# Three maxima products of a cycle in one phase, in the lead of a fused attention and gMLP block

## The chip, the cores and the metric

The kernel runs on one core of a Trainium2 chip. The metric is the time of one execution on the device, in microseconds (us), as the median of several runs. Engines are named as in the profile: PE (matrix products; PEld is its weight loads), DVE (vector), ACT (scalar and activation), POOL (general vector), SP (here only an issuer of DMAs). Each engine works off its own instructions in order; a DMA queue belongs to the engine that issues it.

## What is computed

`x` has 2048 rows of 512. After a layer norm, two branches are computed from it and added to `x`: attention with 32 heads of 16 columns, and a gMLP.

```python
xn = layernorm(x)
qkv = (xn @ wqkv).reshape(B, S, 3, 32, 16)            # q, k, v
p = softmax(einsum("bhqd,bhkd->bhqk", q, k) * 16**-0.5)
A = einsum("bhqk,bhkd->bhqd", p, v).reshape(B, S, 512) @ wo
z = gelu(xn @ w_in); z1, z2 = z[..., :896], layernorm(z[..., 896:])
B_ = (z1 * (einsum("ts,bsf->btf", w_sp, z2) + b_sp)) @ w_out
return x + A + B_
```

## The kernel before

**Numbers in two parts.** Most float32 products are taken as three matmuls of a high and a low part (`mm3`, lines 170 to 172). A high part is a rounding copy on ACT, a low part a subtraction on DVE or POOL; the pair lies in one tile.

**Attention, two heads at a time.** There are 16 head pairs p. Stacks `qst` and `kst` hold the 48 rows of both heads in two halves of the partitions (two heads' matmuls go side by side). For each pair, the softmax needs the row maximum of the scores. So each score is computed twice: once in a *maxima product* (`max_mm`, tile `mx`, L650) with queries on the partitions, which DVE reduces (`max_red`, L658, tile `mm`), and once as a *score tile* (`scores`, tile `st`, L955) with keys on the partitions, in which two more rows of the stacks subtract the maximum; ACT takes the exponential from it (`exp`, tile `pf`), and `pv` multiplies by v (L929). After 16 maxima products `max_fin` (lines 660 to 684) combines their maxima in five small DVE operations into `ms`; `ms` is written to DRAM (`mscr`) by a DMA, and four DMAs load it from there into the rows of `qst`. `mx` and `st` tiles share three accumulator tags, `s0` to `s2`, in turn (`spsum`).

**Phases.** After a prologue (norms, v, the projections of the first four head pairs) the main loop runs over *phases*, the variable `half` in the code. Two phases make a cycle of three score tiles and three maxima products; the maxima run ahead of the scores by LEAD = 27 products. Hence a *lead*: phases -18 to -1, in which there are maxima products only. The first score tile comes in phase 0. In each phase the loop does, in this order:

- `flush()`: DMAs that were put off with `later(k, ...)`, k phases ago, are issued, in the order in which they were put off. They go to SP's queue.
- the score tiles and maxima products of the phase on PE; the exponentials and part of `pv`
- DMAs in `behind` (the writes of `ms`), on ACT's queue
- `max_red` of the phase's products; in even phases `max_fin` of those three products which the counter has reached
- if a group of projection products has ended in the last phase (`drain`): one step of its generator, which copies the accumulator (`qr`, on ACT)
- one step of each generator in `bg`, and of each in `side`, but of `side` only while `load["D"]`, the planner's account of DVE's work, is not above `limit`
- units of the background queue (`qk_rest`, `z2_all`, `z1_all`, ...), four in a phase of the lead (`credit = 2600`, a unit costs 650); later only in odd phases, with a credit that spreads the rest evenly up to score tile 931.

The limit and the account, at the place where the maxima are reduced; `dve(1024)` adds 0.065 + 1024/960 to `load["D"]`:

```python
limit = load["D"] + (2.5 if half % 2 == 0 else 3.0)
for m in ms:
    max_red(m)
...
side[:] = [g for g in side if load["D"] > limit or next(g, 0) is None]
```

**The background of the lead.** `qk_rest` projects q and k for the later head pairs: for each of four row groups g and three column blocks m, a *group* of 12 matmuls for q (a = 0) and one for k (a = 1), four units each. In the lead, groups use two accumulator banks in turn, tags `d` and `o`; from phase -2 on a new (m, g) uses `d` alone. ACT copies a finished group to `qr` (one of four tiles). Then `qk_split` (lines 319 to 330) goes on as a generator in `side`. Its steps: 1. the high part, ACT, into a new tile `hilo` (profile: `qkhl`), of which there are three; 2. the low part, POOL (L325); 3. once the planner's clock for POOL says that this is done, the store to `qscr` or `kscr` is put off by one phase, to SP's queue. A tile is free for its next use when its store has landed. When m = 3 begins, the four xnT pieces of the next row group are fetched by SP (`fetch_xnT`, 512 KB each). The weights of m = 2 and 3 are loaded and split on POOL by the generator `prepare` in `bg`, which hands a weight over when the planner's clock (2.7 per phase) has reached the planner's account of POOL; until then a phase has no group.

Order on every engine is the order in which the code is traced (a schedule by hand); waits are put in for data and for free tiles.

Of the kernel before, what the change touches and what calls it, by code (L numbers as in the profile page):

```python
# [33 lines left out]
LEAD = 27  # L34
# [6 lines left out]
def fused_block(ctx, tc, x, wqkv, wo, w_in, w_spT, b_sp, w_out, out):  # L41
# [48 lines left out]
    mscr = [dr.tile([4, 32, 32], F32, name=f"mscr{i}") for i in range(4)]  # L90
# [16 lines left out]
    now = [-2 * LEAD // 3 - 1]  # L107
# [18 lines left out]
    def later(k, fn, *args):  # L126
        late.append((now[0] + k, fn, args))
# [4 lines left out]
    def flush():  # L132
        due = [l for l in late if l[0] <= now[0]]
        late[:] = [l for l in late if l[0] > now[0]]
        for _, fn, args in due:
            fn(*args)
# [478 lines left out]
    def load_stacks(p, cols=slice(0, S)):  # L615
        m, r = p // 4, (p % 4) * 2
        q, k = qst[p % 2], kst[p % 2]
        sl = [slice((r + j) * DH, (r + j + 1) * DH) for j in range(2)]
        for j in range(2):
            for i, (t, scr) in enumerate(((q, qscr), (k, kscr))):  # L620
                two = t[64 * j:64 * j + 2 * DH, cols], scr[m][sl[j], :, cols]
                one = t[64 * j + 2 * DH:64 * j + KS, cols], scr[m][sl[j], i, cols]
                for args in (two, one):
                    if p and 2 * j + i:
                        later(2 * j + i, move, *args)
                    else:
                        move(*args)
# [4 lines left out]
    behind = []  # L632
# [19 lines left out]
    def max_red(i):  # L652
        if i >= NSTEP:
            return
        p, c, t, kc = step_of(i)
        if i % 16 == 0:
            mmax[i // 16] = at.tile([P, 2, 4, 4], F32, tag="mm", name=f"mm{i // 16}", bufs=2)
        dve(1024).tensor_reduce(mmax[i // 16][:, :, t, kc], mstep.pop(i), AX.X, ALU.max)  # L658

    def max_fin(i):  # L660

        if i < 0 or i >= NSTEP or i % 16 != 15:
            return
        g = i // 16
        p, c = divmod(g, 4)


        mm = mmax.pop(g)
        mn = at.tile([P, 2, 4, 2], F32, tag="mn", name=f"mn{g}", bufs=1)
        mr = mrow[:, 0:16].rearrange("p (j a t) -> p j a t", j=2, a=2)  # L670
        nc.vector.tensor_reduce(mr[:, :, 0, :], mm, AX.X, ALU.max, negate=True)
        nc.vector.tensor_reduce(mn[:, :, :, 0], mm, AX.X, ALU.max, negate=True)
        nc.vector.tensor_reduce(mn.bitcast(F32R)[:, :, :, 1], mm, AX.X, ALU.max)
        with nc.allow_low_precision(reason="the second of two parts, of which the first is exact"):
            nc.vector.tensor_reduce(mr[:, :, 1, :], mn, AX.X, ALU.add)
        ms = at.tile([P, 32], F32, tag="ms", name=f"ms{g}", bufs=2)
        nc.vector.transpose(ms, mrow.bitcast(F32))
        load["D"] += 0.6
        behind.append((now[0] + 1, mscr[g % 4].rearrange("b k x -> (b k) x"), ms))
        for j in range(2):  # L680
            for a in range(2):
                row = 64 * j + KS + a
                k = 4 * (2 * j + a)
                later(2, move, qst[p % 2][row:row + 1, c * 512:(c + 1) * 512], mscr[g % 4][:, k:k + 4, :].rearrange("b t x -> t b x"))
# [121 lines left out]
    def last_mm(t, on):  # L806

        acc = spsum(f"al{t}")
        for a in range(2):
            u = slice(32 * (t % 4 + a), 32 * (t % 4 + a) + 32)  # L810
            nc.tensor.matmul(acc[:, a, :], on[u, :], sel["ones"][u, 1, :], start=True, stop=True)
        return t, acc

    def last_add(t, acc):
        f = fin[t // 2]
        dve(1024).tensor_add(f, acc, f)
        move(out[t * P:(t + 2) * P, :].rearrange("(a p) d -> p a d", p=P), f)
# [9 lines left out]
    def init_rows(a):  # L827

        for j in range(2):
            row = 64 * j + KS  # L830
            for r in range(2):
                nc.gpsimd.dma_start(raw(kst[a])[row + r:row + r + 1, :], cscr[0:1, :])

    engines = {mybir.EngineType.PE, mybir.EngineType.Activation, mybir.EngineType.DVE, mybir.EngineType.Pool, mybir.EngineType.SP}
    with tc.manual_schedule(engines=engines):
# [136 lines left out]
        def exp(n):  # L972
            pf = at.tile([P, 1024], F32, tag="pf", name=f"pf{n}", bufs=PF)
            act(pf, sts.pop(n).rearrange("p j q -> p (j q)"), AF.Exp, 1024, scale=0.25)
            full[n] = pf

        def chunk_out(p, c):
            e = t512(f"e{p}_{c}")
            acc = accs.pop((p, c))
            if (p, c) == order[-1][:2]:  # L980
                act(e[:, 0:256], acc[:, 0:256], AF.Copy, 256)
                dve(256).tensor_copy(e[:, 256:], acc[:, 256:])
            else:
                act(e, acc, AF.Copy, 512)
            if p == NP - 1:
                later(2, lambda: urgent.append(last_pair(c, e)))
                return
            i = (p % 4) * 2
            later(1, move, escr[p // 4][c][i:i + 2].rearrange("j r w d q -> (j r w d) q"), e)
            if p % 4 == 3 or p == NP - 2:  # L990
                later(2, lambda: bg.append(norm_out(p // 4, c)))
# [3 lines left out]
        for half in range(-2 * LEAD // 3, 2 * (N // 3 + 4)):  # L995
            b = 3 * (half // 2)
            ms = [b + LEAD] if half % 2 == 0 else [b + LEAD + 1, b + LEAD + 2]
            ns = [n for n in ([b, b + 1] if half % 2 == 0 else [b + 2]) if 0 <= n < N]
            now[0] = half
            flush()  # L1000
            for n in ns:
                if n == 16:
                    init_rows(1)
                if n % 64 == 14 and n // 64 + 1 < NP:
                    load_stacks(n // 64 + 1)
            pause = max(0, pause - 1.5)
            final = []
            if b + LEAD >= NSTEP and half % 2 and turn and turn[0][0] + 1 in added:
                final.append(last_mm(*turn.pop(0)))
            tiles = [(scores, n) for n in ns]  # L1010
            for i, m in enumerate(ms):
                tiles.insert(1 if half % 2 == 0 else 2 * i, (max_mm, m))
            for make, n in tiles:
                make(n)
            while ended:
                chunk_out(*ended.pop(0))
            for n in ns[:1]:
                exp(n)
            if half % 2 == 0:
                pv_some(b - 1, ready // 2 * 2)  # L1020
            for n in ns[1:]:
                exp(n)
            while behind and behind[0][0] <= half:
                nc.scalar.dma_start(*behind.pop(0)[1:])
            for f in final:
                last_add(*f)
            low = min(load.values())
            for e in load:
                load[e] = min(load[e] - low, 2.0)
# [4 lines that stand above are left out]
            if half % 2 == 0:  # L1034
                for m in range(ms[0] - 2, ms[0] + 1):
                    max_fin(m)
            if drain:
                drain = False
                cost = next(queue[0], None)
                if cost is None:  # L1040
                    queue.pop(0)
                else:
                    pause = -cost
            bg[:] = [g for g in bg if next(g, 0) is None]
            side[:] = [g for g in side if load["D"] > limit or next(g, 0) is None]
            ready += len(ns)
            if b < 0:
                credit = 2600
            elif half % 2:
                credit = min(credit + 3 * (max(todo / max(DENSE - b, 10), 600 if b > DENSE - 15 else 0) if todo > 0 else max((todo + 64 * 650) / max(N - 6 - b, 8), 450)), 3250)  # L1050
            else:
                continue
            if urgent and between and not drain and "ones" in sel:
                queue.insert(0, urgent.pop(0))
                pause = 0
            took = 0
            while queue and not pause and not drain and go():
                cost = next(queue[0], None)
                if cost is None:
                    queue.pop(0)  # L1060
                elif cost <= 0:
                    pause = -cost
                else:
                    drain = between = cost % 1 > 0
                    credit -= cost
                    todo -= cost
                    left[0] -= 1
                    took += 1
# [38 lines left out]
```

## Time and profile before

| | |
|---|---|
| median of 3 runs | 1958.39 us (1957.21 to 1958.47) |
| profiled execution: its own time | 1960.21 us |
| profiled execution: span, first to last instruction | 1958.4 us |
| PE busy | 1938.7 us, 99% of the span |
| DVE, ACT, POOL busy | 1373.7, 1232.5, 725.5 us |
| first maxima product, first score tile | 85.91, 140.44 us |

The page gives for each engine its busy time and share of the span, and the chain of waits: what ended last, followed back. A row of a timeline has the start, the duration (us), the engine (SPq and ACTq are DMA issues), the line, the operation with its output and inputs, how many were merged into the row, and in brackets the idle time of the engine before it and what ended this. A row of the windows view has the length of the stretch, the busy time and count of each engine, the granted clock of PE (1.00 is full), the share of the DMA engines' time, and GB/s. Matmuls overlap, so the difference of two starts says more than one's duration.

### The profile page before, as it was taken

Reading aid. Unit: us, or ns where it says so; the run is one execution under the profiler, and the core shown is the slowest. Engines: PE = TensorE matmul, PEld = TensorE weight load, DVE = VectorE, ACT = ScalarE, POOL = GpSimd, SP = SyncE. Lnnn points to the kernel's source line nnn. Section 1 sums busy time; section 2 is a strip of 40 time slices with the busy share of each in tenths; the row PEclk is TensorE's granted clock in tenths of the full one; section 3 lists DMA queues with packets and bytes.
Section 4 is the critical chain, followed back from the end, with each engine's and each line's share of the span. In section 5 each row is a group of like instructions: output and inputs, shape, how many; then the busy total and the mean of one; then the engine's idle time right before and its main releaser. Section 6 shows DMA issues by size and latency. Waiting matters only on the chain.

```text
span 1958.4 us, 32641 instructions
## 1 busy us (share of the span) xinstructions
PE 1938.7 (99%) x12559; PEld 1049.7 (54%) x12559; DVE 1373.7 (70%) x1565; ACT 1232.5 (63%) x1407; POOL 725.5 (37%) x790
## 2 busy tenths in 40 slices
PE   8999999999999999999999999999999999999998
PEld 7765555555555555555555555555555555555543
DVE  5356777777767677777777767777777777777872
ACT  4347778888677666656566656665666655556664
POOL 3334278889776931026122531017112400002100
PEclk9999999999999999999999999999999999999999
DMA  7566344363535535365545745346454645355323
GB/s 260 201 219 183 104 120 117 111 179 107 144 132 153 183 117 141 101 166 156 142 137 162 202 131 134 104 120 205 110 158 144 180 140 137 106 147 160 105 73 113
DMA packets 229202, 284.23 MB, mean 145 GB/s; under 512 B 35176, under 2 KB 134136, under 8 KB 226168
## 3 DMA queue, kind: packets, MB, share of 16 engines
q1 hardware_dynamic: 217240, 272.64, 47.9%
q0 software_dynamic: 2592, 8.46, 1.1%
q10 hardware_dynamic: 9216, 1.05, 0.4%
q8 instruction: 99, 1.62, 0.3%
q14 instruction: 55, 0.45, 0.1%
HBM read 188.51 MB, written 93.58 MB: 144 GB/s over the span
## 4 chain that ended last, share of the span: by engine, by line
PE 95%; DVE 2%; ACT 1%; issue 1%; DMA 0%; POOL 0%; SPq 0%; DVEq 0%; ACTq 0%
PE o L929 23%; PE mx L650 16%; PE st L955 15%; PE sp L170 7%; PE sp L172 5%; PE sp L171 5%; PE mo L170 2%; PE qk L170 2%; PE z1p L170 2%; PE z2p L170 2%; PE qk L171 1%; PE qk L172 1%; PE mo L171 1%; PE mo L172 1%; PE z1p L172 1%; PE z1p L171 1%
## 5 line engine op out<-in xcount | busy, mean ns | idle before, releaser
L658 DVE TENSOR_REDUCE mm<-mx 128x2 f32<-128x1024 f32 x1024 | 1221.9, 1222 | 498.2 <-PE mx L650 493.9
L58 ACT ACTIVATE pf<-st 128x1024 f32<-128x1024 f32 x1024 | 1028.8, 1025 | 620.0 <-PE st L955 591.6
L929 PE MATMUL o<-pf,vall 128*32 128x512 f32 (+1 forms) x5120 | 511.0, 513 | 0.0
L650 PE MATMUL mx<-kst,qst 48*128 48x512 f32 x2048 | 446.7, 434 | 2.7 <-ACT pf L58 1.8
L955 PE MATMUL st<-qst,kst 50*128 50x512 f32 x2048 | 445.2, 431 | 1.3 <-DVE mm L658 1.1
L650 PEld LDWEIGHTS mx<-kst,qst 48*128 48x128 f32 x2048 | 192.0, 185 | 268.4 <-ACT pf L58 169.6
L955 PEld LDWEIGHTS st<-qst,kst 50*128 50x128 f32 x2048 | 193.1, 185 | 164.0 <-issue 85.7
L929 PEld LDWEIGHTS o<-pf,vall 128*32 128x32 f32 x5120 | 131.4, 109 | 233.5 <-issue 211.5
L170 PE MATMUL sp<-wsp,zs 128*128 128x512 f32 x448 | 193.9, 433 | 0.3 <-DVE z1i L566 0.2
L573 POOL TENSOR_TENSOR z1i<-z1i,hhl 128x512 f32<-128x512 f32 x28 | 36.0, 1287 | 416.1 <-DVE z1i L566 413.3
L172 PE MATMUL sp<-wsp,zs 128*128 128x512 f32 x448 | 176.0, 393 | 0.0
L171 PE MATMUL sp<-wsp,zs 128*128 128x512 f32 x448 | 176.0, 393 | 0.0
L170 PEld LDWEIGHTS sp<-wsp,zs 128*128 128x128 f32 x448 | 83.9, 187 | 68.9 <-issue 51.8
L172 PEld LDWEIGHTS sp<-wsp,zs 128*128 128x128 f32 x448 | 84.1, 188 | 19.9 <-POOL wsp L197 0.5
L171 PEld LDWEIGHTS sp<-wsp,zs 128*128 128x128 f32 x448 | 84.4, 188 | 12.2
L196 POOL CAST wo<-wo0r 128x512 fp32r<-128x512 f32 x1 | 0.6, 612 | 189.6 <-DMA wo0r<-in_wo 189.6
L325 POOL TENSOR_TENSOR qkhl<-qr,qkhl 128x512 fp32r<-128x512 f32 x24 | 30.9, 1289 | 72.1 <-ACT qkhl L58 72.1
L170 PE MATMUL z2p<-w,xt 128*128 128x448 f32 x128 | 51.3, 401 | 0.0
L170 PE MATMUL mo<-wout,hp 128*128 128x512 f32 x112 | 48.5, 433 | 0.6 <-DVE xr L610 0.4
L711 POOL TENSOR_TENSOR ob<-ob 128x512 f32<-128x512 f32 (+1 forms) x16 | 20.6, 1287 | 72.8 <-DMA ob<-rscr 65.7
L172 PE MATMUL z2p<-w,xt 128*128 128x448 f32 x128 | 46.8, 366 | 0.0
L171 PE MATMUL z2p<-w,xt 128*128 128x448 f32 x128 | 46.7, 365 | 0.0
(382 smaller groups left out, 1986.3 us busy)
## 6 DMA issues: line engine op xcount, KB each, us to landing
zs<-z2scr SPq DMA_DIRECT2D x112, 512.0 KB
escr<-e SPq DMA_DIRECT2D x60, 256.0 KB
hscr<-hhl SPq DMA_DIRECT2D x28, 512.0 KB
xscr<-xnT POOLq DMA_DIRECT2D x16, 512.0 KB, 4.8
qscr<-qkhl SPq DMA_DIRECT2D x16, 512.0 KB
kscr<-qkhl SPq DMA_DIRECT2D x16, 512.0 KB
xt<-xscr SPq DMA_DIRECT2D x64, 128.0 KB
z2scr<-z2hl SPq DMA_DIRECT2D x32, 256.0 KB
```

What stands on the lines that cost most here:

```text
L58: return nc.scalar.activation(out, in_, func, **kw)
L170: nc.tensor.matmul(acc, lh, rh, start=first, stop=False)
L171: nc.tensor.matmul(acc, ll, rh, start=False, stop=False)
L172: nc.tensor.matmul(acc, lh, rl, start=False, stop=last)
L196: gps(0.6).tensor_copy(t[:, 0, :n], rw[:, :n])
L325: gps(1.3).tensor_sub(hl[:, 1 - a, :], src, hl[:, a, :].bitcast(F32))
L573: gps(1.3).tensor_add(z1, z1, hl[:, 1, :].bitcast(F32))
L650: nc.tensor.matmul(acc[:, j, :], qst[p % 2][rows, tt * P:(tt + 1) * P], kst[p % 2][rows, kc * 512:(kc + 1) * 512], start=True, stop=True)
L658: dve(1024).tensor_reduce(mmax[i // 16][:, :, t, kc], mstep.pop(i), AX.X, ALU.max)
L711: gps(1.3).tensor_mul(both[rows, 0, :], both[rows, 0, :], both[rows, 2, :])
L929: nc.tensor.matmul(acc[cols:cols + VW, a:a + w], vpack(kt - 1 + r, 2 * p + j), pf[:, j * 512 + a:j * 512 + a + w], start=(kt == 1 and a == ...
L955: nc.tensor.matmul(st[:, j, :], kst[p % 2][rows, kt * P:(kt + 1) * P], qst[p % 2][rows, c * 512:(c + 1) * 512], start=True, stop=True)
```

## The change

In the lead, that is where b < 0, the three maxima products of a cycle are all issued in its even phase; before, one was issued in the even and two in the odd phase. The odd phase of the lead then has none. From phase 0 on the order is the old one. The second edit concerns the write of `ms` to `mscr`: where `max_fin` runs in the lead, the write is put off by one phase to SP's queue with `later`, in place of ACT's queue through `behind`. This applies to the one `max_fin` of the lead, in phase -8. The third edit only keeps the place in the list right where there is no score tile.

```diff
@@ max_fin
-        behind.append((now[0] + 1, mscr[g % 4].rearrange("b k x -> (b k) x"), ms))
+        out_ = mscr[g % 4].rearrange("b k x -> (b k) x"), ms
+        if now[0] < 0:
+            later(1, move, *out_)
+        else:
+            behind.append((now[0] + 1, *out_))
@@ main loop
             ms = [b + LEAD] if half % 2 == 0 else [b + LEAD + 1, b + LEAD + 2]
+            if b < 0:
+                ms = [b + LEAD, b + LEAD + 1, b + LEAD + 2] if half % 2 == 0 else []
@@ main loop
             for i, m in enumerate(ms):
-                tiles.insert(1 if half % 2 == 0 else 2 * i, (max_mm, m))
+                tiles.insert(1 if ns and half % 2 == 0 else 2 * i, (max_mm, m))
```

## The prediction

> **What bounds the kernel now.** I read the page's totals first, then the windows around the stage that the change touches, then the timelines of single engines in that stage. On the page, PE is busy for 99% of the span and holds 95% of the chain of waits, so a microsecond that PE loses or saves anywhere is a microsecond of the kernel.
>
> ```profile
> span 1958.4 us, 32641 instructions
> PE 1938.7 (99%) x12559; PEld 1049.7 (54%) x12559; DVE 1373.7 (70%) x1565; ACT 1232.5 (63%) x1407; POOL 725.5 (37%) x790
> PE 95%; DVE 2%; ACT 1%; issue 1%; DMA 0%; POOL 0%; SPq 0%; DVEq 0%; ACTq 0%
> ```
>
> The stage is the lead: phases -18 to -1, from the first maxima product to the first score tile. In the windows view (PE, PEld, DVE, ACT, POOL busy) PE fills it too, while ACT, DVE and POOL have much time to spare:
>
> ```profile
> 86.00:141.00 55.00, 54.12 (x238) 37.38 (x240) 32.73 (x32) 18.77 (x30) 25.43 (x22) 1.00 0.64 217
> ```
>
> PE's timeline shows how the lead is paid for. "x2" is one maxima product (two half-height matmuls); four L170 rows make one group of 12 projection matmuls (k of one head pair, say).
>
> ```profile
> 85.91 0.50 PE L650 MATMUL mx<-kst,qst 48*128 48x512 f32 x2
> ...
> 92.89 0.97 PE L650 MATMUL mx<-kst,qst 48*128 48x512 f32 x6
> 94.74 0.50 PE L650 MATMUL mx<-kst,qst 48*128 48x512 f32 x2 [0.88 <-DVE mm L658]
> 95.17 0.50 PE L170 MATMUL qk<-xnT,wqk 128*128 128x512 f32 x1
> ...
> 101.72 0.97 PE L650 MATMUL mx<-kst,qst 48*128 48x512 f32 x6
> 102.61 0.50 PE L170 MATMUL qk<-xnT,wqk 128*128 128x512 f32 x1
> 103.41 0.40 PE L170 MATMUL qk<-xnT,wqk 128*128 128x512 f32 x1
> 104.10 0.39 PE L170 MATMUL qk<-xnT,wqk 128*128 128x512 f32 x1
> 104.78 0.39 PE L170 MATMUL qk<-xnT,wqk 128*128 128x512 f32 x1
> 105.56 0.50 PE L650 MATMUL mx<-kst,qst 48*128 48x512 f32 x2
> ...
> 108.90 0.73 PE L650 MATMUL mx<-kst,qst 48*128 48x512 f32 x4
> ...
> 112.52 0.50 PE L650 MATMUL mx<-kst,qst 48*128 48x512 f32 x2
> ...
> 133.46 0.50 PE L650 MATMUL mx<-kst,qst 48*128 48x512 f32 x2
> 133.89 0.50 PE L170 MATMUL qk<-xnT__1212,wqk 128*128 128x512 f32 x1
> ...
> 140.44 0.50 PE L955 MATMUL st<-qst,kst 50*128 50x512 f32 x2
> ```
>
> One product and a group take 3.34 us (105.56 to 108.90), two and a group 3.62 (to 112.52), three and a group 3.84 (101.72 to 105.56). A unit of a group takes 0.685 (103.41 to 104.78 is two), a group alone 2.74. At 92.89 four products stood together, because no projection weights were ready in two phases: the fourth waited for DVE. The lead lasts 54.53 us.
>
> **The change, part by part.** *Order on PE.* A cycle of two phases took 3.34 + 3.62 = 6.96 and takes 3.84 + 2.74 = 6.58, a saving of 0.38 where both phases have a group. But phases -16 to -14 now put six products together. The fourth stands at +1.85 as before (92.89 to 94.74), and each one after it waits for a reduction of 1.16 (below, 3.49 for three): the sixth at 4.17, its group 0.43 later, at 4.60.
>
> *The side list.* This is the part that I expect to decide. Three max_red in an even phase add 3 x 1.13 = 3.4 to load["D"] (the planner's own figures), above its limit of 2.5, so the steps of qk_split, which the side list holds, are skipped in every even phase of the lead. A split then makes one step per cycle: high copy (ACT), low part (POOL) a cycle later, store registered a cycle after that, issued one phase on. Before, the store stood three or four phases behind its copy; now five. The copies write tiles "hilo", of which there are three, so the copy of split n waits for the store of split n-3. Splits 4 and 5 copy in phase -11, 6 and 7 in -9, 8 and 9 in -7; stores 4 and 5 are issued in phase -6, 6 and 7 in -4. Copy 7 thus stands on ACT ahead of what releases its tile, and behind it on ACT stand the evictions of groups 8, 9 and on.
>
> The planner's own clock for POOL also moves: weights (3,1) come out at phase -12 instead of -11, so a sixteenth group fits into the lead. It is 2.74 of PE work taken from later.
>
> *The moved DMA.* The maxima of the first 16 products (the only ones finished in the lead, in phase -8) are written to mscr by SP in phase -7 instead of by ACT. ACT is spared an issue of 0.34 (below), which is worth nothing where it is busy for 18.77 of 55. SP now waits for DVE's ms there, and queued behind are the four qst row loads, stores 4 and 5, four xnT fetches, and store 6. The four loads and what follows them waited for mscr before, too; these are the rows of before on DVE, ACT's queue, SP's queue and ACT:
>
> ```profile
> 102.25 3.49 DVE L658 TENSOR_REDUCE mm<-mx 128x2 f32<-128x1024 f32 x3 [1.24 <-PE mx L650]
> ...
> 114.32 0.19 DVE L671 TENSOR_REDUCE mrow<-mm 128x8 fp32r<-128x32 f32 x1
> ...
> 114.93 0.21 DVE L677 STREAM_TRANSPOSE ms<-mrow 128x32 f32<-128x32 f32 x1
> ```
> ```profile
> 116.67 2.79 SPq L102 DMA_DIRECT2D qst<-mscr  x4
> 119.55 0.56 SPq L102 DMA_DIRECT2D kscr<-qkhl  x1
> 120.22 0.56 SPq L102 DMA_DIRECT2D qscr<-qkhl  x1
> 120.87 0.81 SPq L102 DMA_DIRECT2D xnT__1212<-xscr  x1
> ...
> 124.04 0.53 SPq L102 DMA_DIRECT2D kscr<-qkhl  x1
> ```
> ```profile
> 105.66 0.60 ACT L58 ACTIVATE qr<-qk 128x512 f32<-128x512 f32 x1 [2.47 <-PE qk L172]
> ...
> 115.17 0.34 ACTq L1024 DMA_DIRECT2D mscr<-ms  x1
> ...
> 122.76 0.63 ACT L58 ACTIVATE qkhl<-qr 128x512 fp32r<-128x512 f32 x1 [2.56 <-DMA kscr<-qkhl]
> 123.30 0.58 ACT L58 ACTIVATE qr<-qk 128x512 f32<-128x512 f32 x1
> 125.05 0.63 ACT L58 ACTIVATE qkhl<-qr 128x512 fp32r<-128x512 f32 x1 [1.17 <-DMA qscr<-qkhl]
> ...
> 132.69 0.63 ACT L58 ACTIVATE qkhl<-qr 128x512 fp32r<-128x512 f32 x1 [5.51 <-DMA kscr<-qkhl]
> 133.23 0.58 ACT L58 ACTIVATE qr<-qk 128x512 f32<-128x512 f32 x1
> ```
>
> The kernel of before is already at the edge here: the copy at 132.69 waited 5.51 for a store, the eviction at 133.23 stood behind it, ended at 133.81, and PE took the bank at 133.89, where its own products (133.46 + 0.43) let it start anyway. Its slack was 0.08 us.
>
> *The working, in times of this trace.* Phase -18 at 85.91; -16 at 92.49 (+6.58); its group at 97.09 (+4.60); -12 at 102.78, two groups later (2.95 + 2.74); -10 at 109.36; -8 at 115.94. Group 9 starts 0.89 later (as 101.72 to 102.61), and group 10 could follow at 119.69 (group after a switch 2.86).
>
> First stall. Reductions start 0.53 after the products and take 3.49; the small ones end 0.85 later (114.29 to 115.14): ms is there at 120.81. From the issue of mscr to the qst loads 1.53 (115.14 to 116.67), loads 2.79 and a gap of 0.09: store 4 is issued at 125.22. It lands 3.21 later (119.55 to 122.76): copy 7 at 128.43, eviction 8 at 128.97, done 129.55, PE 0.08 later at 129.63. Groups use two accumulator banks in turn; group 10 needs group 8's. PE stands still from 119.69 to 129.63, **9.94 us**.
>
> Second stall. Copy 9 waits for store 6, which is behind the four xnT fetches. From store 4's issue to that landing it is 13.14 (119.55 to 132.69): 138.36; eviction 10 and PE make it 139.56 for group 12, which PE would reach at 136.21 (129.63 + 2.83 + 0.89 + 2.86). **3.35 us**.
>
> Third, from phase -2 on, groups use one bank. Groups 15 and 16 are now neighbours with no products between: 16 waits for 15's eviction, which ends 3.65 after the group's start (102.61 to 105.66 + 0.60), with PE 0.08 later: 0.87 lost.
>
> Sum: without the two stalls the scores start at 115.94 + 4 x 6.58 + 0.87 = 143.13 instead of 140.44, +2.69, less the group brought forward, -2.74: the order alone is worth nothing, -0.05. The stalls add 13.29. The change costs 13.2 us. The profiled execution took 1960.21 (its span 1958.4), 1.8 above the median of 1958.39; by its own time it becomes 1973.4, by the median **1971.6**.
>
> *What no row shows, bounded.* Store 4's landing: 1.50 (the tiny mscr) to 4.83 (120.22 to 125.05); I take 3.21, the same store in the same place of the queue: -1.7 to +1.6. Store 6's landing: 3.21 to 8.65; I take 8.65, since the same fetches go ahead of it; at 3.21 the second stall is gone. mscr issued by SP: 0 to +0.56, a store's issue; I take 0. The early group: paid back in full or, if later phases had room for it anyway, +2.7.
>
> *The clock.* At the start of the kernel, after a stretch in which PE was mostly idle, eight starts in a row are 0.426 apart instead of 0.23:
>
> ```profile
> 11.68 0.63 PE L170 MATMUL v<-qst,xnT 128*128 128x512 f32 x1
> ...
> 15.09 0.40 PE L172 MATMUL v<-kst,xnT 128*128 128x512 f32 x1
> 15.32 0.40 PE L170 MATMUL v<-qst,xnT 128*128 128x512 f32 x1
> ```
>
> That costs 8 x 0.2 = 1.6. After the first stall it can come again. Group 10 would be slower by 1.6, but group 12 then waits 3.35 - 1.6 for its bank, so the sum is unchanged; it shows only if the second stall is absent. The Trainium skill (TensorE: Matmul & The Clock Gate, "What's actually happening") says that an idle window of about 3.4 us halves the clock and that as much busy time restores it; the 3.41 us of slow starts agree, and by it the dip after 9.94 us of idling is sure rather than possible.
>
> **The rivals.** *No stall.* If copy 7 is not held (store 4 landed by about 118.5, that is ahead of the row loads on SP, or a free tile), evictions run on time and only the order counts: -0.05, 1958.3; were the fifth and sixth product not held by DVE either (0.25 each instead of 1.16) nor group 16 by its bank, 1.8 + 0.87 less, 1955.6. For it speaks that splits in before lived with waits of 5.51 unseen by PE; against it, that this left 0.08. Not slower.
>
> *One stall.* If store 6 lands early, copy 9 is in time, and the clock dip shows: 9.94 + 1.6 - 0.05, or 1969.9 (1968.3 without the dip). For it speaks that fewer bytes are queued after store 6; against it, that what is queued ahead is the same.
>
> *Both stalls, nothing paid back.* If the group brought forward does not shorten the rest, 1974.3. For it speaks that later odd phases are filled by a credit that spreads over hundreds of phases; against it, PE's 99%.
>
> **How the numbers follow.** The forecast 0.64 (own range, the two bounds of store 4 with that of the early group, 1968.2 to 1976.5), no stall 0.13, one stall 0.12, nothing paid back 0.11. The range 1965.5 to 1977.5 holds the first, third and fourth with their bounds and leaves out the second. About 0.2%, 3.9 us, is what a measurement can tell from no change: of no stall, 0.08 falls within it, and 0.05 is left for an order worth more than these rows say, below 1954.5; slower 0.87.
>
> **What would show it.** After: eight visits of products (six together once); mscr<-ms on SP's queue near 121 and the next kscr store near 125; ACT's high copy waiting some 14 us for a kscr store, until about 128; PE idle about 10 us before a projection group near 120 and 3 us near 136, both ended by ACT's eviction; a granted clock below 1 right after; the first score tile near 156.5. It is wrong if copy 7 is in time, if the store waits for something else on SP, or if the steady phases change their length.

## The result and the profile after

The changed kernel takes 1984.66 us (median; 1981.15 to 1986.34), the kernel before 1958.39: 1.0133 times as long, 95% interval 1.0121 to 1.0145. The prediction was 1971.6, with a range up to 1977.5: slower was right, but the loss is 26.3 us by the medians, twice the 13.2 that were predicted.

The totals and the chain of waits on the page of the changed kernel:

```profile
span 1981.1 us, 32634 instructions
PE 1943.6 (98%) x12559; PEld 1054.7 (53%) x12559; DVE 1374.7 (69%) x1566; ACT 1231.6 (62%) x1407; POOL 723.6 (37%) x788
PE 89%; DVE 4%; DMA 4%; POOL 1%; issue 1%; ACT 1%; SPq 1%; DVEq 0%; POOLq 0%; ACTq 0%
```

PE does the same instructions, but 6% of the chain has moved from PE to DVE, DMA and others. The lead on PE's timeline (a group's first row where it waits; "x6" is three products):

```profile
83.55 0.96 PE L650 MATMUL mx<-kst,qst 48*128 48x512 f32 x6
...
90.10 0.96 PE L650 MATMUL mx<-kst,qst 48*128 48x512 f32 x6
...
94.93 0.80 PE L170 MATMUL qk<-xnT,wqk 128*128 128x512 f32 x1
...
102.87 0.97 PE L650 MATMUL mx<-kst,qst 48*128 48x512 f32 x6
109.43 0.96 PE L650 MATMUL mx<-kst,qst 48*128 48x512 f32 x6
115.98 0.97 PE L650 MATMUL mx<-kst,qst 48*128 48x512 f32 x6
129.47 0.80 PE L170 MATMUL qk<-xnT__1038,wqk 128*128 128x512 f32 x1 [9.57 <-ACT qr L58]
134.48 0.97 PE L650 MATMUL mx<-kst,qst 48*128 48x512 f32 x6
138.82 0.50 PE L170 MATMUL qk<-xnT__1038,wqk 128*128 128x512 f32 x1 [0.38 <-ACT qr L58]
...
152.97 0.50 PE L170 MATMUL qk<-xnT__1206,wqk 128*128 128x512 f32 x1 [0.75 <-ACT qr L58]
...
155.92 0.50 PE L959 MATMUL st<-qst,kst 50*128 50x512 f32 x2
```

An undisturbed cycle takes 6.56 (102.87 to 109.43) instead of 6.96, and 9.57 us are lost at once before group 10. ACT's and SP's queues in the same stretch show why:

```profile
113.93 0.62 ACT L58 ACTIVATE qkhl<-qr 128x512 fp32r<-128x512 f32 x1
128.30 0.63 ACT L58 ACTIVATE qkhl<-qr 128x512 fp32r<-128x512 f32 x1 [13.75 <-DMA kscr<-qkhl]
128.83 1.06 ACT L58 ACTIVATE qr<-qk 128x512 f32<-128x512 f32 x2
...
137.65 0.63 ACT L58 ACTIVATE qkhl<-qr 128x512 fp32r<-128x512 f32 x1 [6.53 <-DMA kscr<-qkhl]
```
```profile
120.77 0.33 SPq L102 DMA_DIRECT2D mscr<-ms  x1
122.19 2.80 SPq L102 DMA_DIRECT2D qst<-mscr  x4
125.09 0.56 SPq L102 DMA_DIRECT2D kscr<-qkhl  x1
125.75 0.56 SPq L102 DMA_DIRECT2D qscr<-qkhl  x1
126.40 0.82 SPq L102 DMA_DIRECT2D xnT__1206<-xscr  x1
...
129.62 0.53 SPq L102 DMA_DIRECT2D kscr<-qkhl  x1
```

Copy 7 waits 13.75 us for store 4, which stands on SP behind the write of ms and the four row loads; when it lands, ACT evicts groups 8 and 9, and PE goes on.

The profiled executions are best compared in three parts: up to the first product, the lead (to the first score tile), and the rest (to the end of the span). Each number is a difference of two rows as above.

| | up to first product | lead | rest | median, us |
|---|---|---|---|---|
| before | 85.91 | 54.53 | 1817.96 | 1958.39 |
| changed | 83.55 | 72.37 | 1825.18 | 1984.66 |
| predicted, from the rows of before | 85.91 | 70.5 | 1815.2 | 1971.6 |

The first part holds the same work in both. It varies from one execution to the next (83.2 to 85.5 in the ten experiments below), and the profile of before has a long one; so the spans, 22.7 apart, show 2.4 less than lead and rest together, 25.1. Of these 2.4, 1.6 are the slow stretch near 12 us that the prediction shows for before; in the changed kernel's profile the granted clock is 1.00 from 5 to 20 us. The profiled execution of the changed kernel took 1983.23, 1.4 less than its median. The lead is as predicted within 2 us. The rest has 2.74 less to do and is 7.2 longer.

Where the rest is lost, in the view of who waited for whom, from 200 us to the end (total, times, longest), the changed kernel:

```profile
PE st L959 <- DVE mm L658: 4.2, 11, 0.5
PE mx L650 <- ACT pf L58: 4.1, 5, 2.5
PE mo L170 <- DMA hp<-hscr: 2.8, 1, 2.8
```

and the kernel before:

```profile
PE mx L650 <- ACT pf L58: 1.2, 6, 0.2
PE st L955 <- DVE mm L658: 1.1, 4, 0.4
```

These come to 11.1 against 2.3; other rows of the view are alike in both, apart from 0.7 that only before has: some 8 us more. After the wait for hp, at 1802.9, eight starts stand 0.426 apart, another 1.6. Together that is 9.7 of the 9.96 us by which the rest misses what was predicted.

### The profile page after: what moved, and what is told of

Read it like the earlier page. It is cut to its first block, busy times and chain, and to the rows that moved or that the text cites. A ratio compares the mean times of both kernels' runs of the same rounds, so it can differ in the third digit from the quotient of the medians.

```text
span 1981.1 us, 32634 instructions
## 1 busy us (share of the span) xinstructions
PE 1943.6 (98%) x12559; PEld 1054.7 (53%) x12559; DVE 1374.7 (69%) x1566; ACT 1231.6 (62%) x1407; POOL 723.6 (37%) x788
## 4 chain that ended last, share of the span: by engine, by line
PE 89%; DVE 4%; DMA 4%; POOL 1%; issue 1%; ACT 1%; SPq 1%; DVEq 0%; POOLq 0%; ACTq 0%
PE o L933 22%; PE st L959 14%; PE mx L650 14%; PE sp L170 7%; PE sp L171 5%; PE sp L172 5%; DVE mm L658 2%; PE qk L170 2%; PE z2p L170 2%; PE mo L170 1%; PE z1p L170 1%; PE qk L171 1%; PE qk L172 1%; DMA xr<-in_x 1%; PE z2p L172 1%; PE z2p L171 1%
```

## The experiments

Theory A was what the prediction left after the result: skipped side steps make the stall in the lead, and the group that comes early displaces the later background against the score tiles, where new waits arise. Theory B: whatever is late in the lead stays late in the rest. Theory C: three products in a row cost by themselves.

**Side steps in every phase.** The changed kernel with

```diff
-side[:] = [g for g in side if load["D"] > limit or next(g, 0) is None]
+side[:] = [g for g in side if load["D"] > limit and b >= 0 or next(g, 0) is None]
```

> The changed kernel, but in the lead the side list is advanced in every phase whatever DVE's account says. Theory A (skipped side steps make the stalls; the group that comes early shifts the later background and costs the rest): nothing is skipped, so weights (3,1) come out at phase -11 again and the lead has 15 groups: 3 x 6.58 (first cycle, -10, -9) and four more cycles of 6.58 with 3.84 at -12/-11 and 10.29 for six products and two groups, some 54 to 56 us from the first product to the first score tile (before 54.5, changed 72.4), and the rest as before, 1818 us from the first score tile to the end: about 1958 to 1961. Theory B (lateness in the lead is carried on into the rest) expects the same. Theory C (three products in a row cost by themselves): near 1984.

It takes 1960.54 us, 1.0011 times before (1.0001 to 1.0020). The lead takes 57.50 (83.41 to 140.91), the rest 1818.2. Nearly the whole loss is gone with three products still in one phase: theory C falls. Merged cycles run at their price on PE's timeline:

```profile
105.61 0.96 PE L650 MATMUL mx<-kst,qst 48*128 48x512 f32 x6
112.16 0.97 PE L650 MATMUL mx<-kst,qst 48*128 48x512 f32 x6
118.72 0.96 PE L650 MATMUL mx<-kst,qst 48*128 48x512 f32 x6
125.27 0.97 PE L650 MATMUL mx<-kst,qst 48*128 48x512 f32 x6
130.19 0.50 PE L170 MATMUL qk<-xnT__1214,wqk 128*128 128x512 f32 x1 [0.32 <-DMA xnT__1214<-xscr]
```

The lead is still 3 us longer than before: there are six products together with a slow clock behind them (0.50 from 95 to 97 us), and PE, sooner than before, meets xnT pieces that are not there yet.

**Old order, side steps skipped.** The opposite: the products as before, the skipping alone, with ms written by SP as in the change.

```diff
-side[:] = [g for g in side if load["D"] > limit or next(g, 0) is None]
+side[:] = [g for g in side if load["D"] > limit or b < 0 and half % 2 == 0 or next(g, 0) is None]
```

> The old order of products (one, two), but in even phases of the lead the side list is not advanced, and ms is written by SP as in the changed kernel. Theories A and B: the same blocked copy on ACT, a stall of some 10 us in the lead, sixteen groups, and the rest longer by about 7 us: 1975 to 1986. Theory C: near 1958, since the order is the old one.

It takes 1979.0 us, 1.0102 (1.0087 to 1.0117). The lead takes 67.96 with a stall of 7.3 before the same group, the tenth; the rest takes 1825.4. So most of the loss needs no change of PE's order at all.

**The early group, with and without.** First the changed kernel with the group held back, then the old kernel with the group let through:

```diff
-                while (m, 1) not in wq:
+                while (m, 1) not in wq or m == 3 and now[0] < -11:
```

> The changed kernel, but column block m = 3 of the first row group may not begin before phase -11, so the lead has 15 groups as before. Theory A: stalls of 8 to 13 us stay in the lead, and the rest is as before, 1818 us from the first score tile to the end (the changed kernel: 1825): 1968 to 1975. Theory B: the rest stays as long as in the changed kernel, or longer by the group that is left: 1825 to 1828, 1978 to 1985.

It takes 1971.71 us, 1.0065 (1.0050 to 1.0080), the lead 70.60 and the rest 1816.6. The stall stays (one of 11.4, below), the rest is that of before: lateness in the lead is not carried on, and theory B falls.

```profile
120.50 0.97 PE L650 MATMUL mx<-kst,qst 48*128 48x512 f32 x6
135.83 0.80 PE L170 MATMUL qk<-xnT__1038,wqk 128*128 128x512 f32 x1 [11.42 <-ACT qr L58]
```

```diff
-            gps(1.3).tensor_sub(hl[:, 1 - a, :], src, hl[:, a, :].bitcast(F32))
+            gps(1.3 if now[0] > -12 else 0.0).tensor_sub(hl[:, 1 - a, :], src, hl[:, a, :].bitcast(F32))
```

> The old kernel, but until phase -12 the planner's account of POOL leaves out the low parts of the splits, so that weights (3,1) come out at -12 and a sixteenth group fits into the lead; nothing else is changed. Theory A: the lead takes one group more, 57.3 us, without a stall, and the rest has the waits of the changed kernel, about 1825: 1966 to 1970. Theory B: the rest is shorter by the group, 1815: 1958.

It takes 1970.01 us, 1.0058 (1.0043 to 1.0073). The lead takes 59.76, 2.5 more than expected, of which the view of waits gives 1.2 to xnT pieces and an eviction that were late; the rest takes 1823.6. The same instructions, with nothing but the planner's account changed, lose 11.5 us. The rest is 5.6 longer although it has a group of 2.74 less.

**More tiles.** The splits of the lead take their tiles from the ring of 20 pieces:

```diff
-        hl = hilo(f"qkhl{m}_{a}_{g}")
+        hl = (piece if m and now[0] < 0 else hilo)(f"qkhl{m}_{a}_{g}")
```

> The changed kernel, but in the lead the splits take their tiles from the ring of 20 pieces instead of the three hilo tiles; order and side steps are those of the changed kernel, sixteen groups in the lead. Theory A (the copy on ACT is blocked for want of a tile): no stall before groups 10 and 12, the lead takes some 59 to 61 us (changed 72.4: less 9.6 and the 2.2 of the slow clock behind it), the rest stays near 1825 as in the changed kernel: about 1969 to 1973. Rival (ACT or PE waits for something else on SP's queue): the stall stays, 1982 to 1986.

It takes 1977.41 us, 1.0105 (1.0078 to 1.0133), and its four runs spread from 1973.7 to 1983.7. The wait of ACT for a store is gone, so it was the tile. But the lead is 65.1, not 59 to 61, because SP's queue was the next to be late: the xnT fetch stands behind the same write of ms and came at 127.44. These waits of 1.89 and 1.15 us were followed by another 3.4 us of slow clock (0.50 from 136 to 138).

```profile
130.14 0.96 PE L650 MATMUL mx<-kst,qst 48*128 48x512 f32 x6
132.99 0.47 PE L170 MATMUL qk<-xnT__1206,wqk 128*128 128x512 f32 x1 [1.89 <-DMA xnT__1206<-xscr]
135.08 0.59 PE L170 MATMUL qk<-xnT__1208,wqk 128*128 128x512 f32 x1 [1.15 <-DMA xnT__1208<-xscr]
```

The rest takes 1825.3, with the early group and without the stall on the copy: the early group again.

**The second edit alone.**

```diff
-        behind.append((now[0] + 1, mscr[g % 4].rearrange("b k x -> (b k) x"), ms))
+        out_ = mscr[g % 4].rearrange("b k x -> (b k) x"), ms
+        if now[0] < 0:
+            later(1, move, *out_)
+        else:
+            behind.append((now[0] + 1, *out_))
```

> The second edit alone: the old order of products, the one write of ms in the lead on SP's queue instead of ACT's. Theory A: what waits behind it on SP waited for the same write before, 1958 to 1960. Rival (the write on SP costs by itself): 1965 or more.

It takes 1957.42 us, 0.9996 (0.9986 to 1.0006): it costs nothing by itself.

**The background put back into place.** The changed kernel, in which a turn of the background queue is taken by a stand-in:

```diff
             flush()
+            if half == 1:
+                queue.insert(0, stand_in())
+                todo += 2600.5
...
+        def stand_in():
+            left[0] = ND
+            for c in range(ND):
+                yield 650 + 0.5 * (c == ND - 1)
+            yield 0
```

> The changed kernel, but in phase 1 a stand-in that issues nothing takes the turn of one group from the background queue, and its cost is added to what is left, so that from there PE's order is that of the old kernel again (5987 of its 6541 entries, counted from the end, are the same). Theory A1 (the rest is longer because all background work stands one group earlier against the score tiles): the lead as in the changed kernel, some 72, and the rest 1818 - 2.7 = 1815 us: 1973 to 1976. Theory B (late work from the lead): the rest 1822 or more, 1981 to 1986.

It takes 1977.39 us, 1.0099 (1.0083 to 1.0115), the lead 71.9 and the rest 1819.4 instead of 1825.2. The waits from 200 us on are those of before again, so the place of the background makes them. But the rest did not fall to 1815: with no background in two cycles, PE there waited for ACT and DVE, its clock fell (0.50 from 160 to 170), and 16 products of pv took 2.79 us (1.50 elsewhere). The turn left empty was not saved.

```profile
160.33 0.80 PE L650 MATMUL mx<-kst,qst 48*128 48x512 f32 x2 [0.71 <-ACT pf L58]
...
165.47 0.80 PE L959 MATMUL st<-qst,kst 50*128 50x512 f32 x2 [0.47 <-DVE mm L658]
...
167.32 2.79 PE L933 MATMUL o<-pf,vall 128*32 128x512 f32 x16
```

**The credit alone.** As the last one, without the stand-in: only `todo += 2600.5` in phase 1.

> The changed kernel, but in phase 1 the cost of one group is added to what is left, so that the credit per cycle is that of the old kernel; the group itself stays early. Theory A1 (the shift of the background against the score tiles): the rest stays 1822 to 1828, 1980 to 1986. Theory A2 (the smaller credit per cycle changes the pattern of units): the rest falls to about 1815, 1973 to 1976.

It takes 1985.15 us, 1.0142 (1.0126 to 1.0158), the rest 1830.1. With the credit restored the loss stays, so the smaller credit is not its cause; the shift is left. The waits are others than in the changed kernel: the longest is one of 4.8 us of a score tile for the rows of `qst`, and from inside it on the clock was twice at one half (0.50 from 1807 to 1813 and from 1817 to 1823).

**A group later.** The old kernel, with the group held back one phase more:

```diff
-                while (m, 1) not in wq:
+                while (m, 1) not in wq or m == 3 and now[0] < -10:
```

> The old kernel, but column block m = 3 of the first row group may not begin before phase -10, so the lead has 14 groups, one fewer than the old kernel, and all later background stands one group later against the score tiles. Theory D (the place of the background in the old kernel is a good one, and a shift either way brings waits): the lead some 52 us, the rest 1818 + 2.7 and 5 to 10 us of waits, 1962 to 1969. Rival (only a background that is early collides): the rest 1820.7, 1957 to 1960.

It takes 1962.93 us, 1.0031 (1.0019 to 1.0044), the lead 52.7 and the rest 1825.9: with the 2.7 of a group more, 5.2 are lost. A shift in the other direction costs too, if less. Only some 1.6 of the 5.2 shows as added waits of PE from 200 us on (three new ones for the weights wsp, 2.4 together, others less than before). The remaining 3.6 are mostly slow clock: these waits are of 0.6, 1.2 and 0.6 us, and from the last of them on the windows view gives 0.50 (707 to 713); there 16 products of pv take 2.79 us (at 708.74) instead of 1.50. Some 6.8 us at half speed cost about 3.4.

**Three products in the last three cycles alone**, with side steps in every phase:

```diff
-            if b < 0:
+            if -9 <= b < 0:
                 ms = [b + LEAD, b + LEAD + 1, b + LEAD + 2] if half % 2 == 0 else []
-side[:] = [g for g in side if load["D"] > limit or next(g, 0) is None]
+side[:] = [g for g in side if load["D"] > limit and b >= 0 or next(g, 0) is None]
```

> Three products in one phase only in the last three cycles of the lead (phases -6, -4, -2), with side steps in every phase; before that the old order, so there are neither six products together nor skipped steps, and PE's order from phase 0 on is that of the old kernel (6025 of 6541 entries from the end). If a merged cycle saves 0.38 us wherever nothing is late: 1.1 us, 1956.5 to 1957.5 beside 1958. If the copies on ACT or the fetch of xnT become late for a PE that comes sooner: 1958 to 1960.

It takes 1956.93 us beside 1957.31, 0.9999 (0.9990 to 1.0008). The lead is 53.60 (83.17 to 136.77), 0.9 shorter than before: what merging saves is there, and too small to be told in the whole.

## Why the prediction was wrong

*Right: the mechanism in the lead.* Steps skipped by `load["D"]`, a sixteenth group, copy 7 blocked for a tile, store 4 behind the write of ms on SP. In the trace store 4 is issued at 125.09 (predicted 125.22), copy 7 runs at 128.30 (128.43), PE at 129.47 (129.63), with the first product 2.4 earlier and a slow clock between that gives it back. That these times agree so closely is therefore partly luck; the mechanism is not. The stall is 9.57 (9.94). The old order with skipped steps, the kernel with side steps and the one with more tiles each confirm a link of that chain.

*Sized wrongly in the lead: clock and second stall.* The dip after the first stall was foreseen, at 1.6; it is 2.18 (129.47 to 134.48 is 5.01, where a group and the change to products take 2.83). It was right that it would be hidden by the second stall, which shrank to 0.59 (from 135.37, 0.89 after the products, to 138.82 is 3.45, less 2.86), predicted 3.35; besides the dip, store 6 landed 8.03 after its issue (129.62 to 137.65) instead of 8.65. Another dip was not foreseen: six products with a wait before each of the last three slowed the two groups after them by 2.48 (94.93 to 102.87 and the 0.23 before it, against 5.69). The page of the Trainium skill that the prediction named (TensorE: Matmul & The Clock Gate, "What's actually happening") speaks of an idle window of about 3.4 us; here the longest single gap before the dip was 0.88, so by that rule alone this dip would not have come, and the measurement decides. The windows view of the changed kernel, with the granted clock third from the end:

```profile
89.00:95.00 6.00, 4.15 (x19) 1.95 (x17) 4.34 (x4) 1.23 (x2) 5.84 (x6) 0.83 0.69 193
95.00:100.00 5.00, 5.00 (x13) 3.94 (x13) 2.55 (x3) 0.00 (x0) 0.15 (x1) 0.52 0.96 364
```

The lead came to 72.37 against 70.5.

*Wrong: "the early group ... a group brought forward, less 2.74".* This step failed, and with it the bound that was set for it, 0 to +2.7. The rest has 2.74 us of work less, but it loses 9.96 against what that would give. The prediction took the rest as the same work less one group, since PE is busy for 99%. That share was the result of a place: all background work stands one group earlier against the score tiles, and at some of those places POOL, ACT or SP is now late. These are the two largest waits, on ACT, PE, POOL and SP:

```profile
668.85 0.63 ACT L58 ACTIVATE z<-z 128x512 f32<-128x512 f32 x1 [3.93 <-POOL z L364]
```
```profile
670.44 0.50 PE L650 MATMUL mx<-kst,qst 48*128 48x512 f32 x2 [2.50 <-ACT pf L58]
...
1802.90 0.62 PE L170 MATMUL mo<-wout,hp 128*128 128x512 f32 x1 [2.77 <-DMA hp<-hscr]
```
```profile
649.97 1.30 POOL L715 TENSOR_TENSOR ob<-ob 128x512 f32<-128x512 f32 x1 [3.71 <-DMA ob<-rscr]
...
656.29 0.61 POOL L196 CAST wsp<-wsp_0r 128x512 fp32r<-128x512 f32 x1 [1.94 <-DMA wsp_0r<-in_w_spT]
...
667.55 1.26 POOL L364 TENSOR_TENSOR z<-z 128x512 f32<-128x512 f32 x1
```
```profile
1793.11 1.62 SPq L102 DMA_DIRECT2D os<-escr  x2
1794.78 1.43 SPq L102 DMA_DIRECT2D ob<-escr  x2
1796.27 1.24 SPq L102 DMA_DIRECT2D hp<-hscr  x2
```

POOL in the kernel before, in the stretch that corresponds:

```profile
640.99 0.61 POOL L196 CAST wsp<-wsp_0r 128x512 fp32r<-128x512 f32 x1 [2.00 <-DMA wsp_0r<-in_w_spT]
...
648.62 1.28 POOL L364 TENSOR_TENSOR z<-z 128x512 f32<-128x512 f32 x1
```

At 668.85 ACT waits for POOL, with the exponentials behind it. POOL had itself stood 3.71 and 1.94 us for DMAs, which the planner's clock does not know. That alone is not new: before, it stood 3.00 (at 631.39) and 2.00 us for the same two. New is the work behind the second wait: up to the end of this z it is 12.52 us (656.29 to 668.81), before 8.91 (640.99 to 649.90), because a step of a normalisation (L720) and one more piece of wsp now come in between. This wait of ACT for z also stands in the fourth experiment (4.0), and in none of before, the third and the seventh. At 1796.27 the fetch of hp is issued directly behind the loads of another normalisation on the same queue, and PE was ready for hp 3.9 us later; before, the fetch stood 6.5 us ahead of its product (1774.31 to 1780.84). Smaller waits for hp, of 0.4 to 0.9, stand in the first, sixth and seventh experiment too. That the loss comes from the shift is shown by the parts: with the early group the rest takes 1823.6 to 1830.1, stall or no stall (changed, and the second, fourth, fifth and eighth experiment); without it, 1816.1 to 1818.2, stall or no stall (before, and the first, third, sixth and tenth). That the orders described above cause their own waits is read from the rows, and was not tried by itself.

*The rivals.* "One stall" came nearest in the lead, and with the dip at its price; "nothing paid back" named the right step, with a loss of about a quarter of what came (2.7 against 9.96) and for another reason. "No stall" is close to what the first experiment built: 1960.5, where 1958.3 was given. The merged order is worth as little as the prediction said. The prediction's own range, 1968.2 to 1976.5, does not follow from the bounds named for it: around 1971.6 those of store 4 and of the early group give 1969.9 to 1975.9, and by the prediction's working the second stall would have taken up a shift of store 4 as it does the dip.

## What to carry to other kernels

An edit to a schedule written out by a planner also edits what the planner decides from it: here a DVE account that rose from one reduction to three in the even phases stopped a list of unrelated steps, and that moved a weight by a phase. So the planner's limits are to be worked through first, before any duration, and every unit that changes its phase counts as a change of all that comes after it. And where PE is busy for 99%, that is a property of this alignment: a shift of the background by one group cost several microseconds in either direction here, whatever the work that it moves.

## What the runs showed of the hardware

The granted clock can fall without a long idle time. In the changed kernel it fell to one half at 92.98, after a gap of 0.88 us and inside one of 0.63, and stayed there until 99.80 although PE worked on. The length of the last gap does not tell when: a gap of 2.77 us was followed by eight starts 0.426 apart (1802.90 to 1806.30), but one of 2.50 at 670.44 was not (1.00 from 660 to 700), and in the kernel before neither was the single 0.88 at 94.74 (1.00 from 90 to 98). What does tell is not shown here.

The slow stretches have a grid. In windows of 0.02 us, those of the changed kernel up to 1970 us are 92.98 to 99.80, 123.70 to 133.94 and 1803.06 to 1806.47: two, three and one times 3.41 us, and the second and third start 9 and 501 times 3.4133 us after the first.

Short waits of PE can thus cost more than themselves, and no row names the difference as a wait. In the ninth experiment the clock fell after waits of 0.62 and 1.18 us and inside a third of 0.62, and stayed at one half for 6.8 us. In windows of 60 us from 200 to 1940 us the clock is 1.00 throughout in the kernel before and in the first, third, sixth, seventh and tenth experiment, whose background from there on stands as before. In the changed kernel and in every experiment with a shifted background (second, fourth, fifth, eighth, ninth) one or two of these windows have 0.92 to 0.97.
